# Correcting the TensorE durations from which a kernel's build-time scheduler makes its instruction order

## The chip, the cores and the metric

The kernel runs on one core of one Trainium2 chip. The metric is device time in microseconds (us), median over several executions; lower is better. The kernel is already tuned: the question is what a more truthful build-time model is worth.

## The reference

Eight batches of causal attention with eight heads, 576 tokens of width 64, plus 16 "beacon" keys and values that every token sees, then an MLP with squared ReLU on all 4608 tokens.

```python
# B, H, S, Nb, D = 8, 8, 576, 16, 64 ; d_model 512, d_ff 2048
scores = scale * np.matmul(q, k_all.transpose(0, 1, 3, 2))   # k_all: beacon keys, then keys
a = softmax(where(causal, -1e9, scores))                     # (cut: written out in the source)
attn_out = np.matmul(a, v_all)
x = attn_out.transpose(0, 2, 1, 3).reshape(B * S, H * D)
r = np.maximum(x @ w_in, 0.0)
out = (r * r) @ w_out
```

## The kernel before

The kernel doesn't emit its instructions in program order. It first makes a list of operations (`Op`), each with an engine, a duration in us, dependencies, a priority and buffers that it takes. A greedy list scheduler then simulates the engines: whenever an engine is free in the model, it takes the ready operation of lowest priority number. The instructions are emitted in the order that results. On the chip each engine gets its own list. TensorE doesn't skip ahead in it: in one run below it waits 6.94 us for keys, with other matmuls next in the list that don't need them. So a duration in the model costs nothing on the chip by itself; it decides only who stands before whom.

```python
def add(name, engs, dur, emit, prio, deps, take, give, gate, ...): ...

# Order.run(), cut
while events:
    now = events[0][0]                     # modelled time
    ...                                    # what is done by now releases its users
    for e in engines:
        if free[e] > now: continue
        best = lowest prio among the ready ops whose buffers are free and whose gate is open
                                           # (or, if there is none, one with a closed gate)
        free[e] = now + best.dur           # <- the durations that the change edits
        seen = free[e] + self.LAT[e]       # a DMA: its queue's time plus a landing time
        ...                                # users on TensorE see it op.late later
```

The operations on TensorE that matter here, in blocks that are never split:

```python
# transposes of the beacon keys (4 matmuls)
add(f"tpb{b}", "PE", 0.45, ...)
# transposes of q and k (batches 0 and 1 only; later batches are transposed by DMA)
add(f"tp{b}.{part}.{pr}{xs}", "PE", 0.1 + (0.1 if b == 0 else 0.075) * ns * len(xs), ...)
# scores of one or two pieces of a pair of heads
add(f"qk{p}.{n}.{i}", "PE", 0.24 + cols / 2400.0, ..., gate=gate)
# probabilities times values (AV)
add(f"av{p}.{n}.{heads[0]}", "PE", 0.03 + 0.0325 * nh * sum(t + 1 for t in tl), ...)
# transposes of the attention output into the MLP's x
add(f"xtp{b}.{k}.{pr}", "PE", 0.1 + 0.06 * len(ph.tiles), ...)
# MLP: four matmuls of 512 columns per block (not changed)
add(f"s1.{j}.{ft}.{n}", "PE", 0.865 * N / TCH, ...)
add(f"s2.{j}.{ts}.{qd}", "PE", 0.865, ...)
# transposes of keys and queries by DMA, batches 2 to 7 (not changed); late: TensorE sees them 3 us later
add(f"tr{b}{x}", "SP", 4.1, ..., dma=3.7, late=3.0)
# attention doesn't run ahead of the MLP: its gate opens with MLP work done, not with time
gate = lambda o: o.progress >= 27.7 * (LEAD + PACE * (p - HP))
```

The MLP goes over the tokens in nine chunks of 512. Batch 0 has no MLP work to mix with at first; from about 25 us on, scores, AV and transposes are strewn among MLP blocks.

The softmax here doesn't subtract the row's maximum and nothing guards it: scores larger than these inputs give would overflow.

## Time and profile before

| | before |
|---|---|
| median of 3 first runs | 344.12 us (343.36 to 344.19) |
| span of the profiled run | 342.1 us |
| TensorE busy | 332.1 us, 97% |
| ScalarE, VectorE busy | 191.9 us, 169.4 us |

The page's first part and the chain that ended last (its fourth part, first line):

```profile
PE 332.1 (97%) x2886; PEld 176.4 (52%) x2886; DVE 169.4 (50%) x371; ACT 191.9 (56%) x287; POOL 92.5 (27%) x144
...
PE 85%; DMA 8%; POOL 3%; DVE 2%; ACT 0%; issue 0%; SPq 0%; POOLq 0%; ACTq 0%
```

TensorE binds. But its busy share can't tell how much of the 332 us is work: the Trainium skill, "Trainium Kernel Development and Optimization", section "Performance Expectations", calls matmul busy time a bad metric because matmuls are pipelined. The share is 97%, and waits of half a microsecond hide in it. Better is the time from the end of one block of matmuls to the end of the next. Here are lines of the timeline of TensorE before, cut at 96 us (start, length, engine, line of the kernel, operation, tiles, shapes, count; in brackets idle time and what ended it). L827 is the second MLP product, L792 the first, L661 AV, L609 scores, L729 and L465 transposes. A matmul can start before the one before it ends, so neighbouring lines overlap.

```profile
95.72 1.89 PE L827 MATMUL ps<-w_out,g 128*128 128x512 bf16 x8
98.00 0.58 PE L609 MATMUL strip<-qT,kT 64*128 64x496 bf16 x4 [0.39 <-DMA kT<-qk_area]
98.52 1.04 PE L827 MATMUL ps<-w_out,g 128*128 128x512 bf16 x4
99.39 0.62 PE L661 MATMUL ps<-vb,pt 128*128 128x65 bf16 x15
```

An MLP block ends 0.863 to 0.970 us after its forerunner, an AV block of 15 matmuls 0.45 to 0.57, a score block 0.51 or 0.41. There is one real wait: the first score block of batch 3 waits for keys that a DMA transposes. The chain of waits shows the same place, in order of time (start, length, what):

```profile
86.03 4.36 DMA stg<-in_k_dram
...
91.09 0.98 POOL qk_area L307
92.09 5.86 DMA kT<-qk_area
98.00 0.58 PE strip L609 x4
```

### The profile page before, as it was taken

To read this page: it belongs to the slowest core of one execution; us is meant where nothing else is said; L and a number is where in the kernel's file an instruction comes from. 1 tells how busy PE (TensorE), PEld (TensorE's weight loads), DVE (VectorE), ACT (ScalarE), POOL (GpSimd) and SP (SyncE) were. 2 spreads that over 40 slices of the span, in tenths; PEclk is the share of its full clock that TensorE was granted. 3 is DMA by queue.
4 is the path that set the end of the run, shared out by engine and by line. 5 is a ranking of instruction groups with operands and counts; after the bars stand their busy time and mean duration, and the time that the engine had idled before them with its cause. 6 is when DMAs were issued, how large, how long until landed. Compare 5 with 4: busy or idle time off the path is not lost.

```text
span 342.1 us, 7180 instructions
## 1 busy us (share of the span) xinstructions
PE 332.1 (97%) x2886; PEld 176.4 (52%) x2886; DVE 169.4 (50%) x371; ACT 191.9 (56%) x287; POOL 92.5 (27%) x144
## 2 busy tenths in 40 slices
PE   4999999999999999999999999999999999999995
PEld 2578775444544544445458845444444544444442
DVE  6878975147437863277436643664246502301300
ACT  4776864387766753675347744675557226515611
POOL 9774803324415605041521053014000000000000
PEclk9999999999999999999999999999999999999999
DMA  8999979999999999699989997977210131011002
GB/s 147 210 207 218 206 124 215 209 241 210 193 192 251 245 187 200 145 219 212 208 136 235 158 216 145 229 159 134 86 63 2 24 107 63 0 61 64 0 31 92
DMA packets 143663, 51.68 MB, mean 151 GB/s; under 512 B 130670, under 2 KB 138382, under 8 KB 143630
## 3 DMA queue, kind: packets, MB, share of 16 engines
q1 hardware_dynamic: 135231, 42.25, 62.1%
q0 software_dynamic: 7904, 8.69, 14.8%
q8 instruction: 22, 0.36, 0.5%
q10 hardware_dynamic: 495, 0.30, 0.3%
q14 instruction: 11, 0.09, 0.1%
HBM read 37.22 MB, written 9.44 MB: 136 GB/s over the span
## 4 chain that ended last, share of the span: by engine, by line
PE 85%; DMA 8%; POOL 3%; DVE 2%; ACT 0%; issue 0%; SPq 0%; POOLq 0%; ACTq 0%
PE ps L792 34%; PE ps L827 34%; PE ps L661 8%; PE strip L609 7%; DMA stg<-in_v_dram 3%; DMA kT<-qk_area 2%; DMA stg<-in_q_dram 2%; DMA stg<-in_k_dram 1%; POOL qk_area L430 1%; PE ps L729 1%; POOL qk_area L307 1%; DVE qT L307 1%; DVE g L817 0%; PE ps L465 0%; POOL tri L291 0%
## 5 line engine op out<-in xcount | busy, mean ns | idle before, releaser
L827 PE MATMUL ps<-w_out,g 128*128 128x512 bf16 x576 | 133.8, 379 | 0.0
L792 PE MATMUL ps<-xT,w_in 128*128 128x512 bf16 (+3 forms) x704 | 133.4, 341 | 0.2 <-DVE qT L307 0.2
L624 ACT ACTIVATE pt<-strip 128x832 bf16<-128x832 f32 (+4 forms) x128 | 104.3, 863 | 39.9 <-PE strip L609 39.7
L792 PEld LDWEIGHTS <-w_in 128*128 128x128 bf16 x704 | 65.7, 98 | 56.4 <-issue 4.3
L808 ACT ACTIVATE g<-ps 128x512 bf16<-128x512 f32 (+2 forms) x119 | 67.0, 563 | 41.6 <-PE ps L792 40.9
L827 PEld LDWEIGHTS <-g 128*128 128x128 bf16 x576 | 52.7, 98 | 60.9 <-issue 3.2
L817 DVE TENSOR_TENSOR g<-g 128x1024 bf16<-128x1024 bf16 (+2 forms) x80 | 52.5, 659 | 61.8 <-ACT g L808 59.5
L307 POOL CAST qk_area<-stg 128x512 bf16<-128x512 f32 (+2 forms) x60 | 40.3, 679 | 73.5 <-DMA stg<-in_k_dram 58.8
L305 ACT COPY osb<-ps 128x512 f32<-128x512 f32 x28 | 16.4, 585 | 57.4 <-PE ps L827 51.3
L661 PEld LDWEIGHTS <-pt 128*128 128x128 bf16 (+1 forms) x960 | 37.8, 100 | 14.8 <-issue 3.5
L307 POOL CAST vb<-stg 128x512 bf16<-128x512 f32 (+1 forms) x39 | 26.1, 678 | 62.7 <-DMA stg<-in_v_dram 44.3
L661 PE MATMUL ps<-vb,pt 128*128 128x65 bf16 (+1 forms) x960 | 41.5, 197 | 0.3 <-DVE vb L307 0.3
L609 PE MATMUL strip<-qT,kT 64*128 64x80 bf16 (+6 forms) x400 | 37.3, 292 | 0.4 <-DMA kT<-qk_area 0.4
L681 DVE TENSOR_TENSOR xn<-ps,rcp 128x320 bf16<-128x320 f32 (+2 forms) x64 | 31.5, 492 | 2.3
L635 DVE TENSOR_TENSOR pt<-pt,tri 128x1024 bf16<-128x1024 bf16 (+1 forms) x36 | 23.7, 658 | 15.8 <-ACT pt L624 15.8
L810 DVE TENSOR_SCALAR g<-ps 128x512 bf16<-128x512 f32 (+2 forms) x41 | 24.4, 603 | 14.0 <-PE ps L792 13.5
L679 DVE RECIPROCAL rcp<-ps 128x5 f32<-128x5 f32 (+2 forms) x64 | 12.2, 191 | 34.9 <-PE ps L661 34.7
L609 PEld LDWEIGHTS <-kT 64*128 64x128 bf16 x400 | 12.4, 96 | 17.6 <-issue 12.6
L307 DVE COPY osb<-ps 128x512 f32<-128x512 f32 x8 | 5.5, 692 | 19.1 <-PE ps L827 19.0
L638 DVE TENSOR_TENSOR pt<-pt,tri 80x160 bf16<-80x160 bf16 x32 | 10.3, 320 | 0.0
L352 POOL DMA_DIRECT2D stg<-in_v_dram x10 | 8.5, 850 | 5.0 <-DMA w_in<-in_moe_w_in_dram 3.6
L307 DVE COPY kT<-ps 128x576 bf16<-128x576 bf16 (+3 forms) x11 | 6.5, 594 | 1.9 <-PE ps L465 1.0
(38 smaller groups left out, 64.6 us busy)
## 6 DMA issues: line engine op xcount, KB each, us to landing
out_dram<-osb SPq DMA_DIRECT2D x17, 512.0 KB, 3.9
stg<-in_q_dram SPq DMA_DIRECT2D x24, 256.0 KB, 5.5
stg<-in_k_dram SPq DMA_DIRECT2D x18, 256.0 KB, 5.1
stg<-in_v_dram SPq DMA_DIRECT2D x18, 256.0 KB, 4.6
w_in<-in_moe_w_in_dram POOLq DMA_DIRECT2D x4, 512.0 KB, 8.9
w_out<-in_moe_w_out_dram POOLq DMA_DIRECT2D x4, 512.0 KB, 11.3
stg<-in_v_dram POOLq DMA_DIRECT2D x6, 256.0 KB, 8.3
stg<-in_k_dram SPq DMA_DIRECT2D x6, 224.0 KB, 4.7
```

What stands on the lines that cost most here:

```text
L305: nc.scalar.copy(dst, src)
L307: eng[e].tensor_copy(dst, src)
L609: nc.tensor.matmul(st[:, hj, at:at + t1 - t0], kT[b % 2][hp, pr, 128 * c:128 * c + 128], qT[b % 2][hp, pr, t0:t1], start=True, stop=True,)
L624: nc.scalar.activation(pt[take_pt.held[2]][:, :, off:off + width], st[:, :, 0:width], AF.Exp, bias=0.0, scale=scale)
L635: nc.vector.tensor_tensor(out=d, in0=d, in1=tri[:, m0:m0 + m, :][:, None].to_broadcast([128, 2, m, 128]), op=ALU.min)
L661: nc.tensor.matmul(a[:, at + (t - tl[0]) * (D + 1):at + (t - tl[0] + 1) * (D + 1)], P[0:rr, hj, o:o + 128], vb[b % 2][0:rr, c, 2 * pr + hj ...
L681: nc.vector.tensor_tensor(out=xn[b % 2].rearrange("p t (h d) -> p h t d", d=D)[:, h0:h0 + nh, tl[0]:tl[0] + nt], in0=a[:, :, :, 0:D], in1= ...
L792: nc.tensor.matmul(h[:, lo - spans[0][0]:hi - spans[0][0]], w_in_sb[:, mc, ft * 128:(ft + 1) * 128], xT[:, mc, lo % RING:lo % RING + hi - lo],
L808: nc.scalar.activation(dst, h, AF.Relu, bias=0.0, scale=1.0)
L810: nc.vector.tensor_scalar(out=dst, in0=h, scalar1=0.0, scalar2=None, op0=ALU.max)
L817: nc.vector.tensor_tensor(out=d, in0=d, in1=d, op=ALU.mult)
L827: nc.tensor.matmul(o, G[:, fc, ts * 128:(ts + 1) * 128], w_out_sb[:, fc, :], start=(fc == 0), stop=(fc == NFT - 1))
```

## The change

Intent: the durations of transposes, scores and AV were guesses on the long side; replace them by what the trace shows. Batch 0, which runs at a slow TensorE clock (AV blocks of 24 matmuls take 1.44 and 1.05 us there, then 0.73), gets longer scores and AV; later batches shorter ones. No instruction is added, removed or resized. The whole diff, cut to the durations:

```diff
-  tpb   0.45
+  tpb   0.35 if b == 0 else 0.25
-  tp    0.1 + (0.1 if b == 0 else 0.075) * ns * len(xs)
+  tp    0.05 + (0.1 if b == 0 else 0.047) * ns * len(xs)
-  qk    0.24 + cols / 2400.0
+  qk    (0.2 if b else 0.3) + cols / 2400.0
-  av    0.03 + 0.0325 * nh * sum(t + 1 for t in tl)
+  av    (0.031 if b or (n and p > 1) else 0.05) * nh * sum(t + 1 for t in tl)
-  xtp   0.1 + 0.06 * len(ph.tiles)
+  xtp   0.02 + 0.05 * len(ph.tiles) + (0.1 if b == 0 else 0.0)
```

A warning on reading the start: the clock records of a trace begin with its first rise to full speed (22.47 us in the kernel before), and the granted clock in the views (PEclk) reads 1.00 ahead of that too. There only the length of a known block tells the clock.

More of the change, by code (lines that the diff above doesn't have):

```diff
@@ L412, in add_beacon @@
         busy = [o for pr in range(HP) for o in qk_ops[HP * (b - 2) + pr]] if b >= 2 else []
-        box["t"] = add(f"tpb{b}", "PE", 0.45, emit_tp, prio=prio - 100.0, deps=[bk, ident_op], take=("ps", "tp"))
+        box["t"] = add(f"tpb{b}", "PE", 0.35 if b == 0 else 0.25, emit_tp, prio=prio - 100.0, deps=[bk, ident_op], take=("ps", "tp"))
         def emit_ev(e):
@@ L467, in emit_tp @@
                                                         ident[0:np_, 0:np_])
-                    tp = add(f"tp{b}.{part}.{pr}{xs}", "PE", 0.1 + (0.1 if b == 0 else 0.075) * ns * len(xs), emit_tp,
+                    tp = add(f"tp{b}.{part}.{pr}{xs}", "PE", 0.05 + (0.1 if b == 0 else 0.047) * ns * len(xs), emit_tp,
                              prio=100.0 * (HP * b + pr) - (190 if b else 1190 if part == 0 else 1090) + 0.1 * n,
@@ L614, in emit_qk @@
                             )
-            qk = add(f"qk{p}.{n}.{i}", "PE", 0.24 + cols / 2400.0, emit_qk, prio=base + i - (0.0 if b else 1000.0),
+            qk = add(f"qk{p}.{n}.{i}", "PE", (0.2 if b else 0.3) + cols / 2400.0, emit_qk, prio=base + i - (0.0 if b else 1000.0),
                      deps=qk_deps + [take_pt], take=("strip", "strip", len(group)), gate=gate)
@@ L668, in add_phase @@
             nh = len(heads)
-            av = add(f"av{p}.{n}.{heads[0]}", "PE", 0.03 + 0.0325 * nh * sum(t + 1 for t in tl), emit_av,
+            av = add(f"av{p}.{n}.{heads[0]}", "PE", (0.031 if b or (n and p > 1) else 0.05) * nh * sum(t + 1 for t in tl), emit_av,
                      prio=base - 150 + heads[0] - first,
@@ L730, in emit_tp @@
                                             xn[b % 2][0:n, t, 128 * pr:128 * pr + 128], ident[0:n, 0:n])
-                tp = add(f"xtp{b}.{k}.{pr}", "PE", 0.1 + 0.06 * len(ph.tiles), emit_tp, prio=-120.0 - (500.0 if b == 0 and len(ph.tiles) == 2 else 0.0),
+                tp = add(f"xtp{b}.{k}.{pr}", "PE", 0.02 + 0.05 * len(ph.tiles) + (0.1 if b == 0 else 0.0), emit_tp, prio=-120.0 - (500.0 if b == 0 and len(ph.tiles) == 2 else 0.0),
                          deps=norm_ops[HP * b + pr, k], take=("ps", "tp"))
```

## The prediction

> **What bounds the kernel.** TensorE. The page's first part has it busy 332.1 of 342.1 us (97%), against 56% for ScalarE and 50% for VectorE, and the chain of waits puts 85% of the span on it. Because busy time of pipelined matmuls can hide stalls, I also measured from the end of one block of matmuls to the end of the next, in the timeline of TensorE. After 24 us the block times hardly vary: 4 MLP matmuls of 512 columns 0.863 to 0.970 us, a 15-matmul AV block 0.451 to 0.571, a score block of 4 matmuls 0.51 (one exception, 0.97, at 98 us, a wait for a key transpose by DMA), of 8 matmuls 0.41. MLP is 1152 matmuls of full width, 249 us. Everything above the shortest time of its kind adds up to about 5 us after 24 us, most of it a fixed 0.1 us that the block after a score block pays (0.970 for 0.866). So from 24 us to 338 us an order can win little.
>
> The first 24 us are looser: TensorE starts at 4.3 us, and until some 22 us its matmuls are slow (24-matmul AV blocks took 1.44, 1.05, then 0.73 and 0.74 us). The Trainium skill, "TensorE: Matmul & The Clock Gate", Part 1, has TensorE at half clock until it has been busy for a window; these durations agree. In that stretch ScalarE's exponentials (16 of 0.78 to 0.94 us) and VectorE's copies alternate with TensorE on the chain.
>
> **What the change does.** It adds, removes and resizes no instruction. It only changes the durations with which a greedy list scheduler decides, at build time, the order of instructions on each engine. The new figures fit the trace: AV block 0.52 to 0.465 (trace 0.45 to 0.46), 12 transposes of batch 1 0.55 to 0.33 (trace 0.32 to 0.38), 5 transposes of x 0.40 to 0.27 (trace 0.26), score blocks 0.64 to 0.60 and 0.55 to 0.51 (trace 0.51 and 0.41, plus the 0.1 that the next block pays). Batch 0 gets longer scores and AV, batch 1 on gets shorter. Summed, the scheduler's TensorE time falls by about 8 us (estimate from counts times differences); device time doesn't.
>
> **On the critical path.** The pace of attention against MLP is gated by MLP progress, not by modelled time, and priorities are unchanged, so the order should differ in local swaps: an MLP block before instead of after an AV block or a transpose. Each score block still pays its 0.1 us. Possible gains: about 1 us of stalls in 24 to 110 us (0.45 at 37 us, 0.46 at 98 us), and 0 to 2 us in the start if the swaps fill TensorE earlier. Possible losses are of the same size: a less cautious order makes TensorE wait in order for an exponential, mask or cast that comes late. TensorE's sum of work stays.
>
> **Prediction.** 343.4 us, 80% range 341.4 to 345.2. Faster by over 2%: 0.03; within 2%: 0.94; slower by over 2%: 0.03.
>
> **What would show it.** Same instruction counts per group; TensorE busy within 2 us of 332; end of the last MLP matmul near 337 to 338 us; block times after 25 us as before. First MLP matmul within 2 us of 24.0 us. If 24-matmul AV blocks become fast earlier or later, the start moved the clock, and the time with it.
>
> **What would make it wrong.** The start rearranged so that the clock warms several us earlier or later; a new wait for the DMA-transposed keys or weights of some us; many more or fewer changes between score and MLP blocks; chunks of the MLP shifted so that the end has attention left.

## The result and the profile after

| | before | after |
|---|---|---|
| median, 6 runs each | 343.83 us (343.36 to 344.53) | 343.32 us (343.19 to 344.50) |
| span of the profiled run | 342.1 us | 341.6 us |
| last TensorE matmul ends (trace) | 338.15 us | 337.69 us |
| TensorE blocks in another place | | 82 of 474 |
| end of TensorE in the scheduler's own model | 344.8 us | 338.1 us |

The ratio of the times is 0.9991, with a 95% interval of 0.9973 to 1.0009: the same time; a gain of 0.5 us is not resolved by timing. Ratios here are the mean of one kernel's runs over that of the other's in the same rounds, so not quite the ratio of the medians quoted. "Blocks in another place" counts the blocks that a text comparison of the two TensorE orders finds outside the stretches that agree. The last row is no device time: it is when the scheduler, in its own bookkeeping at build time, thinks that TensorE is done. The 0.46 us in the row of the traces compare one execution with one; the spans of the kernel before differ by 2.3 us between executions (341.1 to 343.4). So what follows explains two traces, not a gain in time.

The page after:

```profile
PE 331.8 (97%) x2886; PEld 175.8 (51%) x2886; DVE 172.0 (50%) x373; ACT 190.2 (56%) x285; POOL 91.7 (27%) x144
...
PE 89%; DMA 6%; POOL 4%; ACT 0%; issue 0%; POOLq 0%; ACTq 0%
```

The timeline of TensorE after, around the same first score block of batch 3 (the one with 64x496 shapes):

```profile
97.32 2.75 PE L827 MATMUL ps<-w_out,g 128*128 128x512 bf16 x12
99.91 0.62 PE L661 MATMUL ps<-vb,pt 128*128 128x65 bf16 x15
100.46 0.58 PE L609 MATMUL strip<-qT,kT 64*128 64x496 bf16 x4
```

It now stands four blocks later in TensorE's list (block 167 instead of 163) and waits for nothing. This wait is the largest single part of the trace's 0.46 us. To see that, I gave each matmul a fixed cost and summed it: for full-height matmuls a column takes 0.417 ns, plus 2.5 ns per matmul (this fits 0.863 us for four of 512 columns and 0.410 us for four of 240), AV 30.2 ns, and scores and the transposes of q and k, which run in pairs, half of their columns (a score block of 1920 columns takes 0.51 us, where 0.417 ns each would make 0.80), with 25 ns at least for those transposes (12 of them take 0.30). The sum is 308.0 us for both kernels. What the clock shows above this sum is time lost:

| lost up to | before | after | difference |
|---|---|---|---|
| 24 us | 15.9 | 16.1 | +0.1 |
| 80 us | 19.5 | 19.2 | -0.4 |
| 100 us | 21.4 | 20.5 | -0.8 |
| 120 us | 22.7 | 22.2 | -0.6 |
| 280 us and to the end | 30.2 | 29.7 | -0.5 |

(At 24 us, where blocks are long, the figures are good to about 0.2 us.) Half of the loss lies in the first 24 us, before the MLP can run, and the change leaves it alone. The rest grows about evenly until the last attention block. Only between 80 and 100 us does one step stand out, and it is the wait for keys.

The place of this block in time explains the change better than the durations themselves. The scheduler put it at 100.8 us of modelled time before; the device was done with the block ahead of it at 97.6 us, 3.2 us early, because the model's TensorE was too slow, and so ahead of the keys' landing. The model's DMA wasn't the culprit: a rerun of the build has these keys landing at 97.4 us (the trace shows 97.95), and adds the `late=3.0` of the code above. TensorE's 3.2 us used up that cushion. After, the scheduler says 101.0 us and the device comes at 100.5 us. The model's TensorE was 2% slow over the whole run and is now right to half a microsecond (338.1 against 337.7 at the end).

The change also moved something on another engine. SyncE issues the five DMA transposes of batch 3's x earlier, with two loads of q behind them that stood before them. Its timeline, before (first two lines) and after:

```profile
128.70 4.88 SPq L352 DMA_DIRECT2D stg<-in_q_dram  x4
133.68 7.82 SPq L712 DMA_TRANSPOSE xT<-xn  x5
129.47 1.93 SPq L352 DMA_DIRECT2D stg<-in_q_dram  x2
131.50 7.46 SPq L712 DMA_TRANSPOSE xT<-xn  x5
```

This will matter below.

### The profile page after: what moved, and what is told of

Read it like the earlier page. It is cut to its first block, busy times and chain, and to the rows that moved or that the text cites. A ratio compares the mean times of both kernels' runs of the same rounds, so it can differ in the third digit from the quotient of the medians.

```text
span 341.6 us, 7198 instructions
## 1 busy us (share of the span) xinstructions
PE 331.8 (97%) x2886; PEld 175.8 (51%) x2886; DVE 172.0 (50%) x373; ACT 190.2 (56%) x285; POOL 91.7 (27%) x144
## 4 chain that ended last, share of the span: by engine, by line
PE 89%; DMA 6%; POOL 4%; ACT 0%; issue 0%; POOLq 0%; ACTq 0%
PE ps L827 37%; PE ps L792 36%; PE ps L661 8%; PE strip L609 7%; DMA qk_area<-in_q_dram 4%; DMA stg<-in_v_dram 2%; POOL qk_area L430 2%; POOL stg L352 1%; PE ps L729 1%; POOL vb L307 0%; PE ps L465 0%; POOL tri L291 0%; POOL w_in L754 0%; ACT osb L305 0%; POOL stg L351 0%; POOL tri L289 0%
## 5 line engine op out<-in xcount | busy, mean ns | idle before, releaser
L827 PE MATMUL ps<-w_out,g 128*128 128x512 bf16 x576 | 133.5, 379 | 0.0
L792 PE MATMUL ps<-xT,w_in 128*128 128x512 bf16 (+3 forms) x704 | 133.1, 341 | 0.0
L792 PEld LDWEIGHTS <-w_in 128*128 128x128 bf16 x704 | 65.5, 98 | 54.8 <-issue 3.6
L808 ACT ACTIVATE g<-ps 128x512 bf16<-128x512 f32 (+2 forms) x116 | 65.4, 564 | 40.4 <-PE ps L792 39.8
L827 PEld LDWEIGHTS <-g 128*128 128x128 bf16 x576 | 53.0, 98 | 60.5 <-issue 2.4
L307 POOL CAST qk_area<-stg 128x512 bf16<-128x512 f32 (+2 forms) x60 | 39.4, 664 | 65.3 <-DMA stg<-in_q_dram 34.4
L661 PEld LDWEIGHTS <-pt 128*128 128x128 bf16 (+1 forms) x960 | 37.1, 99 | 15.1 <-issue 5.0
L810 DVE TENSOR_SCALAR g<-ps 128x512 bf16<-128x512 f32 (+2 forms) x44 | 26.3, 604 | 15.3 <-PE ps L792 14.6
L307 DVE COPY osb<-ps 128x512 f32<-128x512 f32 x9 | 6.2, 692 | 15.7 <-PE ps L827 15.3
L638 DVE TENSOR_TENSOR pt<-pt,tri 80x160 bf16<-80x160 bf16 x32 | 11.1, 348 | 0.0
L305 ACT COPY xT<-ps 128x336 bf16<-128x336 bf16 (+2 forms) x8 | 3.9, 508 | 7.7 <-PE ps L729 7.2
```

Of the source, the lines that this page charges most:

```text
L305: nc.scalar.copy(dst, src)
L307: eng[e].tensor_copy(dst, src)
L661: nc.tensor.matmul(a[:, at + (t - tl[0]) * (D + 1):at + (t - tl[0] + 1) * (D + 1)], P[0:rr, hj, o:o + 128], vb[b % 2][0:rr, c, 2 * pr + hj ...
L792: nc.tensor.matmul(h[:, lo - spans[0][0]:hi - spans[0][0]], w_in_sb[:, mc, ft * 128:(ft + 1) * 128], xT[:, mc, lo % RING:lo % RING + hi - lo],
L808: nc.scalar.activation(dst, h, AF.Relu, bias=0.0, scale=1.0)
L810: nc.vector.tensor_scalar(out=dst, in0=h, scalar1=0.0, scalar2=None, op0=ALU.max)
```

## The experiments

Theory S: from 24 us on TensorE carries a fixed sum of work, and the order can only take away single waits, so better durations are worth about the one wait. Rival C: gains in one half of the change cancel losses in the other. Rival N: the order hardly depends on these figures. Rival T: the order follows true durations and truth pays. All kernels were timed against the kernel before on the same chip, five rounds where five are stated, else three. All outputs are right. Edits are given in short; `old` and `new` are the durations of the diff above.

### Only batch 0, and only batches 1 to 7 (five rounds)

```diff
-  dur = new
+  dur = new if b == 0 else old     # first run
+  dur = old if b == 0 else new     # second run
```

> Only batch 0 gets the new durations. Theory S (TensorE holds a fixed sum of work from 24 us on; the order can only remove single waits): 343.3 to 344.2 us, last TensorE work at 337.5 to 338.5 us, the key wait near 98 us may stay or go. Rival C (a gain in one half of the change cancels a loss in the other): this half is away from before by 1% or more, over 347 or under 340.5 us.

> Only batches 1 to 7 get the new durations; batch 0 keeps the old. Theory S: 343.0 to 344.2 us, within 0.3% of before. Rival C: away by 1% or more in the direction opposite to the run with only batch 0. Both halves within 0.3% would refute C.

Batch 0 alone: 345.77 us (344.88 to 347.59), ratio 1.0065 (1.0037 to 1.0094). Batches 1 to 7 alone: 343.11 us, ratio 0.9983 (0.9959 to 1.0008). Rival C's 1% is not there, but the first half isn't free either: it missed Theory S's range by over 1 us, and with 0.65% it is outside the 0.3% that would have refuted C. So a weaker C isn't refuted: batch 0's half loses something that the whole change doesn't. The timeline of the first run's TensorE has the wait for keys, longer:

```profile
95.74 1.24 PE L827 MATMUL ps<-w_out,g 128*128 128x512 bf16 x5
98.23 0.58 PE L609 MATMUL strip<-qT,kT 64*128 64x496 bf16 x4 [1.25 <-DMA kT<-qk_area]
```

With the longer durations of batch 0 the model's TensorE is slower still: the block stands at place 162, one MLP block earlier than before, and the wait measured from block end to block end grew from 0.56 to 1.42 us, by the 0.86 us of one MLP block. (Both are above half of its columns, 0.40 us and 2.5 ns a matmul; against the 0.51 us that such a block takes elsewhere the first is 0.46, as in the prediction.) With the new durations in batches 1 to 7 it stands at 166, with no wait. So that half alone removes the wait, and batch 0's half pushes the other way: it is the sum of modelled time up to this block that counts. In the trace TensorE ends 1.1 us later than before (339.23); by the sum above 0.4 us of this are lost before 80 us, so not in this wait (full clock is recorded from 23.72 us on, before from 22.47). The median is 2.4 us higher. The profiled execution was the fastest of the six (344.88 us); what the others (345.28 to 347.59 us) lost beyond it is in no trace.

### The same wait, moved by another knob (five rounds each)

```diff
-  tr{b}{x}: dma=3.7, late=3.0
+  tr{b}{x}: dma=3.7, late=5.0      # keys_late: all durations old; early_keys: new ones in batch 0
```

> The kernel before with its old durations; only the modelled latency of the DMA transposes of keys and queries is 5 instead of 3 us, so that the scheduler puts the first score block of a batch later. If the 0.5 us gained by the change came from the lost wait for keys near 98 us, then this kernel has no such wait either and ends 0.3 to 0.6 us earlier than before, at 337.6 to 337.9 us for the last TensorE work, with none of the changed durations. If the gain came from the better durations of TensorE elsewhere, it ends at 338.1 us as before.

> The kernel with the new durations in batch 0 only (which ran at 345.77 us), plus the modelled latency of the DMA transposes of keys at 5 instead of 3 us. In the built order the first score block of batch 3 is block 162 of TensorE with the new durations in batch 0 alone, 163 before, 164 here, 167 after the change; the waits measured there were 1.42, 0.56 and none (after). If those 2 us are the place of this one block, the wait here is 0 to 0.1 us, the last TensorE work ends 1.2 to 1.5 us earlier than without, at 337.7 to 338.1, and the time is 343.2 to 344.3 us. If the loss came from the start, it stays at 345 us or more.

With all the old durations and later keys: TensorE ends at 337.75 us, inside the stated 337.6 to 337.9, without a wait for keys (block 165). So none of the changed durations is needed to lose that wait or for an end this early. But the hit on the number is partly luck: by the sum above this trace is 1.4 us ahead of the one before at 100 us, 0.9 of it already at 80 us, and gives 0.96 us back in a new wait near 140 us. The timing can't resolve it: 343.69 us, ratio 1.0011 (0.9989 to 1.0033).

With the new durations of batch 0 and later keys the expectation was missed: 345.13 us, ratio 1.0035 (1.0014 to 1.0056), TensorE ends at 338.81. The wait for keys is gone, but TensorE, now earlier at the first MLP block of chunk 3, waits there for another DMA transpose, that of x. The timeline of its TensorE:

```profile
139.17 1.04 PE L827 MATMUL ps<-w_out,g 128*128 128x512 bf16 x4
141.37 1.02 PE L792 MATMUL ps<-xT,w_in 128*128 128x512 bf16 x4 [1.15 <-DMA xT<-xn]
```

So 1.4 us were won and 1.3 us of them (block end to block end; some records of matmuls are missing from this trace) given back 40 us later. The kernel with all old durations and late keys has the same wait, 0.96 us:

```profile
140.31 1.02 PE L792 MATMUL ps<-xT,w_in 128*128 128x512 bf16 x4 [0.80 <-DMA xT<-xn]
```

In both, SyncE issues these transposes late (from 134.69 and 133.52 us). The wait for keys had been hiding this: the kernel before, at 133.68 us no earlier, gets to the block only at 140.87 us and doesn't wait. The change (131.50) and its half for batches 1 to 7 (130.29) issue them earlier and have no wait here either. That this is why they keep what they won is argued from the traces; no run moved the transposes alone. The cause of the 2 us of the first run is therefore this pair of DMA waits only in part; the run-to-run part stays open, since there is one trace per kernel.

### Durations wrong by a factor of two

```diff
-  dur = new
+  dur = 0.5 * new                   # short_half, all five kinds
+  dur = 2.0 * new                   # long_double
```

> All five changed durations are half of the new ones, so wrong by 2 on purpose (the scheduler's own TensorE time falls further). Rival T (the order follows true durations, and truth pays): clearly slower, by 1% or more. Theory S: the order moves many more blocks than the change did, but TensorE always finds ready work: under 0.6% slower, 343 to 346 us. Rival N (the order hardly depends on these figures): same order and same time to 0.1%.

> All five changed durations are twice the new ones. The scheduler then believes that TensorE is slow, so that exponentials look early beside it. Theory S: 0.2 to 1.5% slower, 344.5 to 349 us, by waits of TensorE for exponentials or masks. Rival T: slower by 2% or more. Rival N: same as before to 0.1%.

Half: 351.00 us, ratio 1.0218 (1.0188 to 1.0247), 205 blocks moved. Twice: 362.63 us, ratio 1.0553 (1.0522 to 1.0585), 130 blocks moved. Rival N falls: the order does depend on these figures. Theory S was too strong as well: it expected under 0.6% and under 1.5%. Both results are as Rival T forecast (1% and 2% or more). What speaks against T is that truer durations didn't pay: not in the change itself, and less than nothing in batch 0 alone. Twice the durations makes the model's TensorE far too slow: the first score block of batch 2 is planned for 84.6 us, the device reaches it at 64 us and waits until the keys land. Its timeline of TensorE:

```profile
63.32 0.63 PE L661 MATMUL ps<-vb,pt 128*128 128x65 bf16 x15
70.89 0.98 PE L609 MATMUL strip<-qT,kT 64*128 64x496 bf16 x4 [6.94 <-DMA kT<-qk_area]
71.81 0.66 PE L729 MATMUL ps<-ident,xn 112*128 112x112 bf16 x5
72.27 4.44 PE L827 MATMUL ps<-w_out,g 128*128 128x512 bf16 x12
```

Twelve matmuls of L827 take 4.44 us there, where the changed kernel takes 2.75. That is the clock. The windows view of this kernel (stretch, its length, then busy us and count of TensorE, its weight loads, VectorE, ScalarE and GpSimd, then granted clock, DMA share and GB/s) has it at half (0.50) from within the wait on; of the 19.2 us by which TensorE ends later than before, 16.1 are lost between 24 and 80 us:

```profile
60.00:68.80 8.80, 3.95 (x46) 2.35 (x44) 3.61 (x9) 0.40 (x2) 3.79 (x6) 1.00 1.04 196
68.90:75.60 6.70, 4.71 (x17) 1.81 (x18) 0.46 (x1) 1.83 (x2) 0.95 (x2) 0.50 1.04 201
```

In the kernel with halved durations the clock falls after a stretch from 104 to 110 us in which attention blocks stood in TensorE's list without MLP blocks between them, several of them waiting for an exponential, a mask or a normalisation. Of the 8.3 us by which its TensorE ends later than before, 5.9 are lost between 100 and 120 us. Its windows:

```profile
104.00:110.40 6.40, 3.90 (x79) 2.63 (x77) 4.82 (x13) 3.46 (x5) 1.67 (x3) 1.00 1.14 233
110.50:113.80 3.30, 3.30 (x18) 1.32 (x19) 0.46 (x1) 2.17 (x4) 1.46 (x3) 0.50 1.29 204
```

The Trainium skill, "TensorE: Matmul & The Clock Gate", Part 1, says that TensorE falls to half clock after an idle window of about 3.4 us and climbs back after a busy one; both traces agree in the factor (0.50), and the times at half above are one and two such windows long in the clock records (3.41 and 6.83 us). The wait of 6.94 us is an idle window of that kind; the second trace has none (longest idle time 1.15 us), so there the page's rule doesn't cover the fall.

### Exponentials wrong by a factor of two

```diff
-  exp  0.18 + 2 * width / 1200.0
+  exp  0.5 * (0.18 + 2 * width / 1200.0)     # exp_half
+  exp  2.0 * (0.18 + 2 * width / 1200.0)     # exp_double
```

> The kernel after the change, with the exponentials modelled at half of their duration (wrong in the direction in which the scheduler expects their results too early). Theory S: TensorE now waits in order for exponentials: waits of some 0.3 us each at part of the 128, 1 to 4% slower, 347 to 358 us. If a wrong ScalarE figure is as harmless as a wrong TensorE figure: within 0.3%, 343 to 344.5 us.

> The kernel after the change, with the exponentials modelled at twice their duration (too cautious). Theory S: TensorE is filled with MLP blocks meanwhile; attention lags and the start is stretched: 0 to 2% slower, 343.3 to 350 us, with few new waits of TensorE after 30 us.

I had it the wrong way round. Too short: 344.47 us, ratio 1.0023 (1.0008 to 1.0038), although 172 blocks moved. Too long: 366.98 us, ratio 1.0671 (1.0649 to 1.0692). A cautious model is not a safe one. It holds attention back (the last AV block of batch 3 ends at 152.8 us, after the change at 129.2), and what hangs on attention late in the chain (the transposed x of the next MLP chunk) is then missing when nothing else is left to do, as the timeline of TensorE with doubled exponentials shows:

```profile
154.61 0.37 PE L609 MATMUL strip<-qT,kT 64*128 64x464 bf16 x2 [0.16 <-ACT pt L624]
155.34 1.09 PE L661 MATMUL ps<-vb,pt 128*128 128x65 bf16 x30 [0.36 <-DVE pt L635]
159.07 5.30 PE L792 MATMUL ps<-xT,w_in 128*128 128x512 bf16 x16 [2.63 <-DMA xT<-xn]
```

Waits of first MLP matmuls for x add up to 5.7 us there, and the clock drops twice. Why halved exponentials hurt so little was not tried further.

### One score piece per block

```diff
-  SINGLE = ()
+  SINGLE = range(32)        # on top of the change
```

> The kernel after the change, with score blocks of one piece instead of two in every pair, so 112 instead of 56 score blocks after batch 0. If what is lost after 24 us (14 us by my count of block times) is mostly a fixed cost of each change from a score block to a full-width block, about 0.1 to 0.2 us, then 56 more such changes cost 6 to 11 us: 349 to 355 us. If it is waits that an order could remove, smaller blocks free strips sooner and it is no slower than 344.5 us.

348.60 us, ratio 1.0143 (1.0124 to 1.0162); TensorE ends at 342.30 us, 4.6 us after the changed kernel. This is just under the stated range, and what was mis-sized is the count: 33 of the 112 score blocks after batch 0 are followed by another score block, so there are 79 changes to another kind of block, 23 more and not 56. No new wait over 0.25 us appears after 24 us. Of the 13.7 us that the changed kernel loses after 24 us, the blocks behind score blocks hold 6.0 by block ends (56 times about 0.107, as in 0.970 for 0.863 us), and the score blocks themselves 6.4 above half of their columns. Here the first is 8.3 us (79 times 0.106) and the second 9.0 us (112 times 0.08). So both grow with their counts, and neither is a wait. Of the first, an order could save only by putting score blocks side by side.

### The start: TensorE kept busy while it has nothing to do

```diff
+  ones = w_out_sb[:, 0, :]; nc.vector.memset(ones, 1.0)   # that tile is loaded much later
+  add_busy("busy0", 7, -2000.0)       # 7 (busy7) or 16 (busy16) matmuls of 512 columns, result unused
```

> The kernel after the change, plus 7 matmuls of 512 columns on a tile of ones before the first transpose (3 us at the slow rate, in time in which TensorE had nothing to do). If the slow TensorE of the first 22 us is a matter of its having been idle, AV blocks of 24 matmuls become 0.73 us earlier, and the time falls by 0.5 to 3 us, to 340.5 to 343 us. If 3 us of work are too little to change the rate, the same as after: 343.3 us to 0.3 us.

> The same with 16 such matmuls (6.8 us at the slow rate, so the first transposes start some 3.5 us late unless the rate rises on the way). The rate rises before the first transposes. If the start is held by slow TensorE, the loss of 2 to 3 us is more than given back: 340 to 343.5 us. If it is held by ScalarE, VectorE and loads, it isn't: 345 to 347 us.

7 matmuls: 343.83 us, ratio 0.9994 (0.9967 to 1.0021), between the two stated ranges. The AV blocks of 24 matmuls became fast (0.73 us) at 21.4 instead of 22.2 us and MLP work stood 0.66 us ahead at 27.1 us. Then TensorE gave it back, waiting for the loads of batch 1, in the timeline of the kernel with 7 matmuls:

```profile
27.09 1.86 PE L803 MATMUL ps<-xT,w_in 128*128 128x240 bf16 x16
29.60 0.70 PE L476 MATMUL ps<-ident,qk_area 96*64 96x96 bf16 x24 [0.65 <-DMA qk_area<-in_k_dram]
```

(Eleven added lines shift the numbers: L803 is L792, L476 is L465.) 16 matmuls: 348.63 us, ratio 1.0144 (1.0116 to 1.0172), over both stated ranges. The clock rose at 6.5 us, but the late start made the scheduler put all transposes of batch 0 ahead of the first scores; TensorE waited 3.2 us for VectorE's copies, and at 13.3 us the clock fell back to half.

Would it have held with a better place for the transposes of batch 1? (five rounds)

```diff
-  loads of batch 1: late 1.5
+  loads of batch 1: late 2.5          # with the 7 matmuls
```

> The kernel after the change with the 7 extra matmuls in the idle time at the start (these made MLP work start 0.7 us earlier, and TensorE gave it back in a wait for the loads of batch 1 at 29.6 us), plus those loads modelled 1 us later, so that two more MLP blocks come before the first transposes of batch 1. If the gain was lost in that wait alone, the wait is gone and TensorE ends at 336.9 to 337.4 us, 342.4 to 343.2 us in all, 0.2 to 0.3% under before. If later waits take it back too, TensorE ends at 337.6 us or later.

No: 344.25 us, ratio 1.0003 (0.9983 to 1.0023), TensorE ends at 338.44 us. The wait at 29.6 us is gone as planned, but in this trace the start itself went differently: the clock was full from 5.7 to 9.1 us, fell back in a wait of 1.36 us, and rose again only at 22.8 us. Windows of this kernel:

```profile
5.80:9.00 3.20, 2.16 (x42) 1.38 (x42) 3.05 (x8) 1.85 (x3) 3.20 (x5) 1.00 1.09 151
9.40:22.60 13.20, 12.17 (x152) 7.28 (x153) 9.13 (x24) 9.52 (x13) 11.01 (x15) 0.50 1.17 212
```

The kernel with 7 matmuls and unchanged loads has the same list for TensorE up to 30 us, and its early blocks were slow throughout until 19.6 us (12 transposes at 7.8 us took 0.45 us here, at 8.3 us 0.69 there). The mean granted clocks of all runs show that it varies within one kernel too: 0.978 in one of four runs with 7 matmuls and 0.980 in two of six with later loads (an estimate from these: some 14 to 15 us at half), and 0.997 to 1.000 in the others. It doesn't decide the time: the run at 0.978 was the fastest of its four (343.06 us), and the two at 0.980 (344.10, 343.63) lie within the spread of the rest (343.15 to 344.96). No kernel here is resolved as faster than the kernel before.

### All kernels together

The kernels with extra matmuls and with single score pieces, told of above, are left out.

| kernel | blocks moved | TensorE end in the model | TensorE end in the trace | time ratio to before |
|---|---|---|---|---|
| before | 0 | 344.8 | 338.2 | 1 |
| after | 82 | 338.1 | 337.7 | 0.9991 |
| batch 0 alone | 59 | 345.6 | 339.2 | 1.0065 |
| batches 1 to 7 alone | 75 | 338.7 | 337.6 | 0.9983 |
| old, keys later | 34 | 345.0 | 337.8 | 1.0011 |
| batch 0 alone, keys later | 61 | 345.8 | 338.8 | 1.0035 |
| half durations | 205 | 319.0 | 346.4 | 1.0218 |
| double durations | 130 | 417.8 | 357.4 | 1.0553 |
| half exponentials | 172 | 337.6 | 338.7 | 1.0023 |
| double exponentials | 204 | 369.4 | 363.1 | 1.0671 |

## Why the prediction was right

It said 343.4 us and "within 2%"; the median is 343.32 us. That it is within 0.1 us is luck: the kernel before alone has medians of 343.40 to 343.89 us in the groups of rounds. That nothing but single waits could move is what was understood.

- "It adds, removes and resizes no instruction": right; the counts on TensorE are the same 2886, and busy time moved from 332.1 to 331.8 us.
- "The scheduler's TensorE time falls by about 8 us; device time doesn't": right. The model's end fell by 6.7 us, the device's by 0.46 us in the trace and by nothing that timing resolves.
- "Possible gains: about 1 us of stalls in 24 to 110 us (0.45 at 37 us, 0.46 at 98 us)": right in place. The wait at 98 us went; its removal in another way gave the same end of TensorE, though with more won before and a new wait after. At 37 us no wait is left, but a smaller one came (0.2 us at 34 us). The "0 to 2 us in the start" didn't come.
- "So from 24 us to 338 us an order can win little": right, and consistent with the cost found in and behind each score block. The figure of "about 5 us" lost there was counted against the shortest block of each kind; against the columns it is 14 us, mostly at score blocks and right behind them.
- "Possible losses are of the same size": right for errors of this size, not in general. Durations wrong by two cost 0.2 to 7%. The prediction gave no such limit.
- "The start rearranged so that the clock warms several us earlier or later": it was rearranged a little, and of the AV blocks of 24 matmuls one is slow instead of two (1.93 us, then 0.73 from 22.2 us on). Full clock is recorded from 21.50 us on, before from 22.47. Yet the first MLP matmul starts at 24.66 instead of 23.99 us, within the 2 us stated, and the loss up to 24 us is the same to 0.2 us. So the clock moved by 1 us, but "the time with it" didn't.
- "A less cautious order makes TensorE wait": the change did the opposite for the keys. Shorter durations of TensorE put score blocks later relative to DMA. The doubled exponentials show that caution about the other engines costs more than haste.

## What to carry to other kernels

When a list scheduler makes the order, a shorter modelled time is not a gain; compare its clock with the trace at the places where two engines or a DMA meet, because it is the accumulated error there, not the error of one duration, that turns into a wait. If the bounding engine is already fed, correcting durations by a few per cent in sum is worth only the waits that can be named in the trace beforehand (here one, 0.5 us), and one taken away may uncover the next. Look then at every engine's list: the change moved DMA transposes as well. Errors of a factor of two are another matter, and the worst of them here was a model that is too cautious about an engine which doesn't bind.

## What the Trainium skill lacked or had wrong

- "TensorE: Matmul & The Clock Gate" (the table "Why this matters for your kernels") advises against gaps of TensorE over about 3 us. In the kernel with halved durations TensorE's longest idle time from 104 to 110 us was 1.15 us, it was busy for 3.90 of 6.40 us, and the clock still fell to 0.50 for 3.41 us. The page's section on micro-idles between groups tells of such oscillation for another pattern, but gives no limit in length or share.
- "TensorEngine Tiling (Array Packing)", section "Key Properties", lacks the time that a change of tiling mode takes. Going from score matmuls on 64 rows to full-height ones, 0.863 us became 0.970 us for the next block: 0.107 us in 56 changes, 0.106 in 79. That the change of mode is the reason is not shown.
- "TensorE: Matmul & The Clock Gate" (Part 1) says that the moment of warming varies from run to run. These traces agree, and with waits between the first blocks the size is larger than the page's half a microsecond: with the same list for TensorE, full clock from 19.6 us in one trace, and in another from 5.7 to 9.1 us and then from 22.8 us.
